# Local and global attention with a gated layer behind it: who normalises the probabilities of batches 2 to 7

## The chip, the cores and the metric

The kernel runs on one core of one Trainium2 chip. The core has five engines with a queue each, which work through their instructions in order: TensorE (PE, its weight loads PEld), VectorE (DVE), ScalarE (ACT), GpSimd (POOL) and SyncE (SP), which here issues every DMA. What counts is the time of one execution in microseconds on the device; lower is better.

## The reference

Per batch and head (8 x 8, head size 64), 512 local queries attend to 32 global keys and to the local keys within 32 positions; 32 global queries attend to all 544 keys. The softmax has an epsilon of 1e-9 in its denominator. The rows of all heads are put side by side (512 numbers for each of 4352 tokens) and go through a layer of width 2048:

```
def _moe_ref(x, w_in, w_out):
    h = x @ w_in
    g = h * np.cos(h)
    return g @ w_out
```

Inputs and result are fp32.

## The kernel before

**Two planes.** TensorE is fed with 16-bit floats. Every fp32 operand is scaled and split in two of them, a high plane (the rounded value) and a low plane (the remainder), and a product is three matmuls: high by high, high by low, low by high.

**The matrix layer** runs over 17 chunks of 256 tokens (`c`; two per batch, and a last one for the global queries of all batches), each in 8 slots (`j`), 136 slots in all. In a slot, 24 matmuls make `ph` (L877, 128 x 512 in PSUM, three buffers); ACT and DVE reduce the angle (`u`, L899 and L900); ACT takes the sine (`w`, L421), POOL squares it in place (L912), DVE makes `gf` from it and `ph` (L914), ACT casts its high plane `gh` (L918), POOL subtracts for the low plane `gl` (L919). Three slots later twelve matmuls (L933 to L935; L935 is the one that reads `gl`) add the result into two tiles `po`, one for each 128 tokens. At the end of a chunk ACT copies out the first `po` (L943) and DVE the second (L941), and SP writes them. A `ph` tile needs the buffer that the `gf` three slots earlier has read.

**The attention** of later batches runs in the same stretch, in pairs of heads: four pairs per batch, one in every four slots, so that the normalising of pairs 0 and 2 falls to slot 0 of a chunk and that of pairs 1 and 3 to slot 4. For a pair SP loads q and k (`qkr`, one buffer, L432), DVE takes their maximum (L472), TensorE spreads it (L454), ACT and DVE make the planes (`qa` L511, `kl` L512), SP copies halves of them (L521 to L526). The scores of four tiles of 128 queries come by TensorE (L579, L580); DVE scales them, adds the mask and takes the minimum (L596, two heads separately); ACT takes exponentials in place in `t` and sums them into `sm` (L421). Then `sc_d` normalises the four tiles and writes their planes into four fixed buffers `planes`, SP transposes these (`pt`, L688), and TensorE multiplies with the planes of v (L721; `vh` L569, `vl` L570, `vr` loaded at L439, its maximum at L540). Every second pair also has the global queries' scores (`gt`, `planes_g` L799, `ptg` L803). The result becomes `xh` (L745) and `xl` (L746), input of the matrix layer one batch later.

`sc_d` has several ways to normalise, chosen by a number: batch 0 by a list per tile, batch 1 by `PL1` (3), later batches by `PL` (1).

**Order.** The program writes the steps in an order by slot and phase; the tool that builds the kernel then reorders the instructions of each engine's queue by a timeline of its own. So a changed instruction can move others.

Of the kernel before, what the change touches and what calls it, by code (L numbers as in the profile page):

```python
# [45 lines left out]
SB = 2.0**14  # L46
T0 = 3
QB = 0
PL = 1
MF = 1  # L50
TS = 1
CH = ''
# [81 lines left out]
def body(tc, qk, v, wi, wo, mask, out):  # L134
# [5 lines left out]
    with ExitStack() as ctx:  # L140
# [504 lines left out]
        def sc_d(b, p, i):  # L645
# [3 lines left out]
            w = WIN[i][1]  # L649
            pl = PLS[i] if b == 0 else (PL0, PL1, PL)[min(b, 2)]  # L650
            if b < 2 and DEFN[b]:
# [504 lines left out]
```

## Time and profile before

| | |
|---|---|
| median of 3 runs | 1051.38 us (1048.57 to 1051.77) |
| the profiled execution | 1045.26 us, its span 1043.5 us |
| PE busy | 879.3 us (84%) |
| DVE busy | 729.4 us (70%) |
| ACT busy | 707.9 us (68%) |
| POOL busy | 463.1 us (44%) |
| granted TensorE clock, mean | 0.941 |

The profile is of one execution. A group's row reads: line, engine, operation, output <- inputs, output shape <- input shape, count, then total busy time and mean ns of one, then the idle time before such instructions and what ended it. A row of the timeline starts with its start and its length in us; the idle time before it and its releaser stand in brackets. Batches 0 and 1 of the attention, the loads and the splitting of the weights fill the first 250 us or so; from there to 884 us batches 2 to 7 run beside chunks 1 to 12, and the rest is matrix layer alone.

### The profile page before, as it was taken

The numbers are of one execution on the slowest core, as the hardware profiler recorded it, in microseconds if no ns is written. First come the engines' busy times: TensorE is split into PE (matmuls) and PEld (weight loads), VectorE is DVE, ScalarE is ACT, GpSimd is POOL, SyncE is SP. The second block draws the span as 40 slices with busy tenths as digits, with TensorE's granted clock in tenths as the row PEclk, the third lists the DMA queues.
The fourth block names the chain that finished last, engine by engine and source line by source line (L and its number), as shares of the span: only waits on it lengthen the run. The fifth ranks groups of instructions, "written<-read, shape, count | busy, mean of one in ns | idle before, by whom it ended". The sixth has DMA issues, their size and how long they took to land.

```text
span 1043.5 us, 20761 instructions
## 1 busy us (share of the span) xinstructions
PE 879.3 (84%) x7819; PEld 600.3 (58%) x7819; DVE 729.4 (70%) x1797; ACT 707.9 (68%) x1458; POOL 463.1 (44%) x396
## 2 busy tenths in 40 slices
PE   2133558677999999999899998999889999999996
PEld 1112435455566666666666666666667676666663
DVE  5997598999577777786777777877777766433231
ACT  6676478887378776877677667876777777434342
POOL 4885285957334342434233333333334333444442
PEclk9955679887999999999999999999999999999998
DMA  9869622796464546354553545455555442200000
GB/s 368 213 202 218 179 99 89 157 178 127 115 131 89 130 83 162 86 122 90 155 106 94 116 123 108 111 107 145 106 105 102 110 85 63 46 21 21 1 21 21
DMA packets 181565, 120.18 MB, mean 115 GB/s; under 512 B 159832, under 2 KB 159832, under 8 KB 179416
## 3 DMA queue, kind: packets, MB, share of 16 engines
q1 hardware_dynamic: 181464, 118.85, 47.6%
q8 instruction: 61, 1.00, 0.4%
q14 instruction: 40, 0.33, 0.1%
HBM read 51.81 MB, written 8.91 MB: 58 GB/s over the span
## 4 chain that ended last, share of the span: by engine, by line
DVE 36%; PE 29%; DMA 14%; ACT 11%; issue 6%; POOL 2%; SPq 1%; ACTq 0%; DVEq 0%; POOLq 0%
PE ph L877 12%; DMA qkr<-qk 6%; DVE t L596 5%; DVE planes L676 5%; PE po L933 5%; PE po L935 5%; PE po L934 5%; DVE u L900 4%; DMA vr<-v 3%; DVE gf L914 3%; ACT L421 3%; DVE kl L512 2%; DVE qm L472 2%; PE acc L721 2%; DVE vl L570 2%
## 5 line engine op out<-in xcount | busy, mean ns | idle before, releaser
L877 PE MATMUL ph<-xh,wi_h 128*128 128x256 f16 x1024 | 281.8, 276 | 31.1 <-DVE gf L914 31.1
L877 PE MATMUL ph<-xl,wi_h 128*128 128x256 f16 x1024 | 282.3, 276 | 0.0
L877 PE MATMUL ph<-xh,wi_l 128*128 128x256 f16 x1024 | 282.2, 276 | 0.0
L919 POOL TENSOR_TENSOR gl<-gf,gh 128x512 f16<-128x512 f32 x136 | 165.1, 1218 | 234.0 <-ACT gh L918 233.6
L912 POOL TENSOR_TENSOR w<-w 128x512 f32<-128x512 f32 x136 | 145.6, 1075 | 266.5 <-ACT w L421 254.5
L877 PEld LDWEIGHTS <-wi_h 128*128 128x128 f16 x2176 | 211.6, 99 | 68.1 <-DVE gf L914 18.4
L933 PE MATMUL po<-wo_h,gh 128*128 128x512 f16 x544 | 206.9, 384 | 21.3 <-DVE o L941 17.7
L934 PE MATMUL po<-wo_l,gh 128*128 128x512 f16 x544 | 207.2, 381 | 0.6 <-POOL wo_l L268 0.6
L935 PE MATMUL po<-wo_h,gl 128*128 128x512 f16 x544 | 206.9, 381 | 0.0
L421 ACT ACTIVATE w<-u,ca 128x512 f32<-128x512 f32 x136 | 97.0, 721 | 112.6 <-DVE u L900 112.2
L900 DVE SCALAR_TENSOR_TENSOR u<-u,cm,ph 128x512 f32<-128x512 f32 x136 | 100.0, 742 | 97.1 <-ACT u L899 97.0
L421 ACT ACTIVATE t<-t,mn 128x192 f32<-128x192 f32 (+1 forms) x256 | 117.1, 458 | 59.3 <-DVE mn L596 58.8
L918 ACT CAST gh<-gf 128x512 f16<-128x512 f32 x136 | 83.1, 611 | 78.0 <-DVE gf L914 70.6
L914 DVE SCALAR_TENSOR_TENSOR gf<-w,ph 128x512 f32<-128x512 f32 x136 | 92.5, 681 | 55.2 <-POOL w L912 55.0
L877 PEld LDWEIGHTS <-wi_l 128*128 128x128 f16 x1088 | 107.6, 99 | 15.7 <-issue 2.0
L596 DVE CUSTOM_DVE_ANT_0 t<-ps,msk,al 128x192 f32<-128x192 f32 (+1 forms) x256 | 99.5, 426 | 10.4 <-PE ps L580 10.3
L899 ACT ACTIVATE u<-ph,cm 128x512 f32<-128x512 f32 x136 | 92.1, 677 | 16.5 <-PE ph L877 16.5
L934 PEld LDWEIGHTS <-gh 128*128 128x128 f16 x544 | 53.4, 98 | 69.6 <-issue 21.2
L676 DVE SCALAR_TENSOR_TENSOR planes<-t,sm,planes 128x192 f16<-128x192 f32 (+1 forms) x192 | 83.9, 489 | 10.7 <-ACT planes L673 10.7
L935 PEld LDWEIGHTS <-gl 128*128 128x128 f16 x544 | 53.4, 98 | 64.3 <-issue 1.7
L933 PEld LDWEIGHTS <-gh 128*128 128x128 f16 x544 | 53.2, 98 | 54.0 <-issue 5.3
L421 ACT ACT_TABLE_LOAD x57 | 73.1, 1283 | 1.0
(183 smaller groups left out, 1428.4 us busy)
## 6 DMA issues: line engine op xcount, KB each, us to landing
qkr<-qk SPq DMA_DIRECT2D x29, 608.0 KB, 4.6
vr<-v SPq DMA_DIRECT2D x8, 1280.0 KB, 7.8
kh<-qa SPq DMA_DIRECT2D x62, 152.0 KB, 2.6
out<-o SPq DMA_DIRECT2D x34, 256.0 KB, 2.6
qa<-kl SPq DMA_DIRECT2D x31, 152.0 KB, 3.7
kl<-kl SPq DMA_DIRECT2D x31, 152.0 KB, 4.7
wo_h<-wi SPq DMA_DIRECT2D x4, 1024.0 KB, 7.9
raw_wi<-wi SPq DMA_DIRECT2D x4, 1024.0 KB, 10.7
```

Of the source, the lines that this page charges most:

```text
L421: ins = nc.scalar.activation(*a, **k).ins
L596: nc.vector.tensor_tensor_reduce(t[:, h], pt[:, h], msk[:, MOFF[i] : MOFF[i] + w], al, 3.0e38, ALU.add, ALU.min, mn[:, h : h + 1],)
L676: nc.vector.scalar_tensor_tensor(lo, t[:, h], r, hi, op0=ALU.mult, op1=ALU.subtract)
L877: nc.tensor.matmul(ph[:, a], w[:, kc, f], x[:, kc, q], start=first and ip == 0, stop=last and ip == 2, skip_group_check=True,)
L899: nc.scalar.activation(u, ph, AF.Identity, bias=m)
L900: nc.vector.scalar_tensor_tensor(u, u, m, ph, op0=ALU.subtract, op1=ALU.subtract)
L912: nc.gpsimd.tensor_tensor(w, w, w, op=ALU.mult)
L914: nc.vector.scalar_tensor_tensor(gf, w, 0.5, st.pop(("ph", c, j)).rearrange("p a b -> p (a b)"), op0=ALU.subtract, op1=ALU.mult,)
L919: nc.gpsimd.tensor_tensor(gl, gf, gh, op=ALU.subtract)
L933: nc.tensor.matmul(po[k], gh[:, q], wo_h[:, f], start=(f == 0), stop=False)
L934: nc.tensor.matmul(po[k], gh[:, q], wo_l[:, f], start=False, stop=False)
L935: nc.tensor.matmul(po[k], gl[:, q], wo_h[:, f], start=False, stop=(f == NJ - 1))
```

## The change

One number: batches 2 to 7 take way 3 of `sc_d`, as batch 1 does, instead of way 1.

```diff
-PL = 1
+PL = 3
```

What `sc_d` does for a tile of `w` = 192 or 224 keys and two heads, cut to the two ways (`rr` holds the reciprocals of the sums):

```
649  w = WIN[i][1]
...
653  if pl in (0, 3, 4, 5):
654      if pl == 3:
655          r = rr[:, 2 * i : 2 * i + 2]
656          rb = bass.AP(tensor=r.tensor, offset=r.offset, ap=[r.ap[0], (1, 2), (0, w)])
657          nc.gpsimd.tensor_tensor(t, t, rb, op=ALU.mult)
...
665      (nc.scalar.copy if pl != 5 or HIE[i] else nc.vector.tensor_copy)(hi, t)
666      nc.gpsimd.tensor_tensor(lo, t, hi, op=ALU.subtract)
667  else:
668      for h in range(2):
...
673          nc.scalar.activation(hi, t[:, h], AF.Identity, scale=r)
...
676          nc.vector.scalar_tensor_tensor(lo, t[:, h], r, hi, op0=ALU.mult, op1=ALU.subtract)
```

Way 1 was, for each head, one ACT operation (L673: times the reciprocal, high plane) and one DVE operation (L676: times the reciprocal, less the high plane). Way 3 is, for both heads at once, a POOL multiplication in place (L657), an ACT cast (L665) and a POOL subtraction (L666). Over 6 batches, 4 pairs and 4 tiles that is 192 operations less on DVE, 96 less on ACT (192 gone, 96 new) and 192 more on POOL. Nothing else in the program text differs; the queues' orders do, from slot 16 on.

The first place is slot 3 and 4 of a chunk (here chunk 8; pair 1 of batch 5 is normalised, and `t_1_0` to `t_1_2` are its tiles). POOL before:

```order
L912 TENSOR_TENSOR w_3_7817<-w_3_7817 128x512
L799 TENSOR_TENSOR planes_g<-gt_0_7550,planes_g 128x544
L919 TENSOR_TENSOR gl_3_7915<-gf_3_7917,gh_3_7914 128x512
L912 TENSOR_TENSOR w_4_7947<-w_4_7947 128x512
L912 TENSOR_TENSOR w_5_8028<-w_5_8028 128x512
```

POOL now, where the numbers behind the names are others for the same tiles:

```order
L657 TENSOR_TENSOR t_1_0_7498<-t_1_0_7498,sm_1_7849 128x384
L657 TENSOR_TENSOR t_1_1_7585<-t_1_1_7585,sm_1_7849 128x448
...
L912 TENSOR_TENSOR w_3_7765<-w_3_7765 128x512
L799 TENSOR_TENSOR planes_g<-gt_0_7502,planes_g 128x544
L666 TENSOR_TENSOR planes_76<-t_1_0_7498,planes_76 128x2x192
...
L666 TENSOR_TENSOR planes_82<-t_1_2_7722,planes_82 128x2x192
L912 TENSOR_TENSOR w_4_7895<-w_4_7895 128x512
L919 TENSOR_TENSOR gl_3_7863<-gf_3_7865,gh_3_7862 128x512
L912 TENSOR_TENSOR w_5_7972<-w_5_7972 128x512
```

The four multiplications stand before w_3, the four subtractions before w_4, and gl_3 behind w_4. (Beside the even pairs, at slot 0, the multiplications stand behind w_7. For pair 0 then come gl_7, the four subtractions, w_0, w_1 and gl_0; for pair 2 w_0, a subtraction, gl_7, three subtractions, gl_0, w_1.) DVE at the same place, before:

```order
L512 SCALAR_TENSOR_TENSOR kl_3_8053<-qkr_3_7779,qs_3_7893,qa_3_8052 128x1216
L914 SCALAR_TENSOR_TENSOR gf_3_7917<-w_3_7817,ph_3_7791 128x512
L676 SCALAR_TENSOR_TENSOR planes_76<-t_1_0_7546,sm_1_7901,planes_76 128x192 x2
...
L900 SCALAR_TENSOR_TENSOR u_4_7946<-u_4_7946,cm_7476,ph_4_7921 128x512
L900 SCALAR_TENSOR_TENSOR u_5_8027<-u_5_8027,cm_7476,ph_5_8002 128x512
...
L914 SCALAR_TENSOR_TENSOR gf_4_7998<-w_4_7947,ph_4_7921 128x512
L914 SCALAR_TENSOR_TENSOR gf_5_8061<-w_5_8028,ph_5_8002 128x512
L900 SCALAR_TENSOR_TENSOR u_6_8090<-u_6_8090,cm_7476,ph_6_8065 128x512
L472 TENSOR_REDUCE qm_0_8225<-qkr_0_8125 128x1
```

DVE now:

```order
L512 SCALAR_TENSOR_TENSOR kl_3_7997<-qkr_3_7727,qs_3_7841,qa_3_7996 128x1216
L900 SCALAR_TENSOR_TENSOR u_4_7894<-u_4_7894,cm_7428,ph_4_7869 128x512
L596 ISA t_2_0_7915,mn_2_0_7916<-ps_2_0_7910,msk,al_2_7415 128x192
...
L914 SCALAR_TENSOR_TENSOR gf_3_7865<-w_3_7765,ph_3_7739 128x512
L472 TENSOR_REDUCE qm_0_8169<-qkr_0_8069 128x1
L900 SCALAR_TENSOR_TENSOR u_5_7971<-u_5_7971,cm_7428,ph_5_7946 128x512
L448 TENSOR_SCALAR d_qk_0_8171<-ident,qm_0_8169 128x128
...
L914 SCALAR_TENSOR_TENSOR gf_4_7942<-w_4_7895,ph_4_7869 128x512
L900 SCALAR_TENSOR_TENSOR u_6_8034<-u_6_8034,cm_7428,ph_6_8009 128x512
```

L676 is gone; u_4 and the next pair's score reductions (L596) stand before gf_3, and L472, the maximum over the next q and k, stands before u_5 and gf_4. On SP the load behind L472 moved as well: it stood behind the transposes of the pair's planes and stands now before them, right behind the copies `kh`.

The second place is TensorE around the product of tile 3. Before, its twelve matmuls stood together ahead of `ph_7`. Now:

```order
L933 MATMUL po_1_7769<-wo_h,gh_3_7862 128x512
...
L934 MATMUL po_1_7769<-wo_l,gh_3_7862 128x512
...
L579 MATMUL ps_2_2_8052<-kh_2_7594,qa_2_7590 128x224
...
L721 MATMUL acc_1_8122<-pt_1_8057,vh_1_7403 64x128
...
L877 MATMUL ph_7_8079<-xh_6288,wi_h 128x256
...
L877 MATMUL ph_7_8079<-xl_6289,wi_h 128x256
...
L935 MATMUL po_0_7768<-wo_h,gl_3_7863 128x512
```

Four of the twelve come first; then four score matmuls, eleven of the attention's product (`acc_1`, which stood behind the product of tile 4), and two of `ph_7`; the remaining eight, four of which read gl_3, come behind those.

The third place is DVE before the chunk boundary in the chunk of pair 2 (here chunk 9). Before:

```order
L914 SCALAR_TENSOR_TENSOR gf_1_8494<-w_1_8389,ph_1_8363 128x512
...
L512 SCALAR_TENSOR_TENSOR kl_0_8424<-qkr_0_8125,qs_0_8235,qa_0_8423 128x1216
...
L570 SCALAR_TENSOR_TENSOR vl_2_9443<-vr_8176,vs_8350,vh_2_9442 128x640
L900 SCALAR_TENSOR_TENSOR u_2_8523<-u_2_8523,cm_7476,ph_2_8498 128x512
L472 TENSOR_REDUCE qm_1_8662<-qkr_1_8560 128x1
L941 TENSOR_SCALAR o_1_8541<-po_1_7821,co_7477 128x512
```

Now:

```order
L512 SCALAR_TENSOR_TENSOR kl_0_8364<-qkr_0_8069,qs_0_8179,qa_0_8363 128x1216
...
L570 SCALAR_TENSOR_TENSOR vl_2_9375<-vr_8120,vs_8290,vh_2_9374 128x640
L914 SCALAR_TENSOR_TENSOR gf_1_8434<-w_1_8329,ph_1_8303 128x512
L900 SCALAR_TENSOR_TENSOR u_2_8463<-u_2_8463,cm_7428,ph_2_8438 128x512
L941 TENSOR_SCALAR o_1_8481<-po_1_7769,co_7429 128x512
...
L472 TENSOR_REDUCE qm_1_8602<-qkr_1_8500 128x1
```

gf_1 moved behind the last L570, and L941 ahead of L472. In the chunk of pair 0, L472 still stands ahead of L941, and gf_0 moved ahead of L512.

## The prediction

> **What bounds the kernel now.** I read the view by windows first. Batches 2 to 7 of the attention, where the change lies, run beside the matrix chunks between 250 and 884 us; behind that stand chunks 13 to 16 alone. The row gives the stretch, the busy time (and count) of PE, its weight loads, DVE, ACT and POOL, then the granted clock and the DMA share.
>
> ```profile
> 250.00:884.00 634.00, 602.07 (x5600) 413.59 (x5600) 465.70 (x1221) 465.49 (x995) 232.00 (x205) 0.99 0.50 111
> ```
>
> TensorE is busy 602.07 of 634 us at full clock. So 31.9 us is all that any relief of DVE and ACT can win here, and POOL is the idlest engine (37%). Next I read the waits between 260 and 900 us (line waited for, total us, times, longest), because they say where those 31.9 us lie.
>
> ```profile
> PE po L933 <- DVE o L941: 17.7, 11, 2.7
> PE ph L877 <- DVE gf L914: 10.6, 8, 1.5
> DVE qm L472 <- DMA qkr<-qk: 43.1, 20, 3.4
> ```
>
> Two places hold 28.3 us of it. The first is the chunk boundary: the second half of a new chunk's `po` needs the old one copied out by DVE (L941), and DVE stands in front of it at the maximum over the next q and k (L472), which waits for their load. The second is the pair of `ph` tiles 6 and 7 of some chunks: they need the `ph` buffers of tiles 3 and 4, which are free once DVE has made gf_3 and gf_4 (L914). The timeline of one even chunk (8) shows the second:
>
> ```profile
> 624.62 2.33 DVE L512 SCALAR_TENSOR_TENSOR kl<-qkr,qs,qa 128x1216 f16<-128x1216 f32 x1 [1.68 <-ACT qa L511]
> 626.88 0.67 DVE L914 SCALAR_TENSOR_TENSOR gf<-w,ph 128x512 f32<-128x512 f32 x1
> 627.60 0.27 PE L877 MATMUL ph<-xh,wi_h 128*128 128x256 f16 x1 [1.53 <-DVE gf L914]
> 634.59 0.28 PE L877 MATMUL ph<-xh,wi_h 128*128 128x256 f16 x1 [1.23 <-DVE gf L914]
> 633.84 0.69 DVE L914 SCALAR_TENSOR_TENSOR gf<-w,ph 128x512 f32<-128x512 f32 x1 [0.56 <-POOL w L912]
> 634.79 0.57 SPq L432 DMA_DIRECT2D qkr<-qk  x1
> ```
>
> Every `ph` tile 6 and 7 is that close. In chunks 4, 6, 8 and 10 TensorE waits there; in the other eight (chunk 9 below) it has about 2.2 us in hand for gf_3 (678.86 to 681.10) and 0.85 for gf_4 (685.85 to 686.70):
>
> ```profile
> 678.19 0.67 DVE L914 SCALAR_TENSOR_TENSOR gf<-w,ph 128x512 f32<-128x512 f32 x1
> 681.10 0.27 PE L877 MATMUL ph<-xh,wi_h 128*128 128x256 f16 x1
> 685.16 0.69 DVE L914 SCALAR_TENSOR_TENSOR gf<-w,ph 128x512 f32<-128x512 f32 x1 [0.57 <-POOL w L912]
> 686.70 0.27 PE L877 MATMUL ph<-xh,wi_h 128*128 128x256 f16 x1
> ```
>
> **Prices.** Batch 1 already runs the new form, so its operations stand in the trace (groups of 160 to 260 us for POOL, of the whole run for ACT and DVE):
>
> ```profile
> L657 POOL TENSOR_TENSOR t<-t,sm 128x448 f32<-128x448 f32 x8 | 7.9, 1003 | 0.0
> L657 POOL TENSOR_TENSOR t<-t,sm 128x384 f32<-128x384 f32 x8 | 7.3, 918 | 2.7 <-DVE sm L643 2.7
> L666 POOL TENSOR_TENSOR planes<-t,planes 128x384 f16<-128x384 f32 x8 | 10.4, 1294 | 1.0 <-ACT planes L665 1.0
> L666 POOL TENSOR_TENSOR planes<-t,planes 128x448 f16<-128x448 f32 x8 | 9.6, 1208 | 0.0
> L665 ACT CAST planes<-t 128x448 f16<-128x448 f32 x16 | 8.7, 558 | 0.0
> L673 ACT ACTIVATE planes<-t,sm 128x224 f16<-128x224 f32 x96 | 38.0, 466 | 0.0
> L676 DVE SCALAR_TENSOR_TENSOR planes<-t,sm,planes 128x192 f16<-128x192 f32 (+1 forms) x192 | 83.9, 489 | 10.7 <-ACT planes L673 10.7
> L919 POOL TENSOR_TENSOR gl<-gf,gh 128x512 f16<-128x512 f32 x136 | 165.1, 1218 | 234.0 <-ACT gh L918 233.6
> ```
>
> For each of 24 pairs (four tiles), DVE loses eight operations of 0.489, 3.9 us (83.9 in all by the row, where they overlap a little), and ACT exchanges two activations of 0.466 for one cast of 0.558, four times. POOL gains four multiplications (2 x 0.918 + 2 x 1.003 = 3.84 us) and four subtractions (2 x 1.294 + 2 x 1.208 = 5.00 us), 212 us in all, so it goes from 232 to some 444 of 634 us (70%). No engine's total passes TensorE's. What counts is where the blocks of 3.84 and 5.00 us stand in POOL's queue, since w (L912) feeds gf and gl (L919) feeds the second product; and what the changed orders do. The orders are those shown under the change.
>
> **Odd pairs (1 and 3), beside gf_3 and gf_4.** The reciprocal of the sums is ready at 621.45 and POOL is idle then:
>
> ```profile
> 621.25 0.20 DVE L643 RECIPROCAL sm<-sm 128x8 f32<-128x8 f32 x1
> 623.46 1.04 POOL L912 TENSOR_TENSOR w<-w 128x512 f32<-128x512 f32 x1 [8.54 <-ACT w L421]
> qkr<-qk SPq DMA_DIRECT2D x29, 608.0 KB, 4.6
> 664.74 0.38 PE L934 MATMUL po<-wo_l,gh 128*128 128x512 f16 x1
> 664.96 0.38 PE L935 MATMUL po<-wo_h,gl 128*128 128x512 f16 x1
> 346.83 1.29 PE acc L721 x36
> ```
>
> Multiplications to 625.3, w_3 to 626.3 (now 624.5), planes_g to 627.5, subtractions to 632.5, w_4 to 633.6, gl_3 to 634.8. On DVE L512 ends at 626.9 as now, but the new order puts u_4 (0.7, of L941's kind and size) and two score reductions (0.7 together, of half that size each) ahead of gf_3: it ends at 628.9, not 627.5, and the wait at 627.60 grows from 1.53 to 2.9 us. Behind gf_3 now stands L472, which used to come after gf_4 and gf_5. SP issues its load right after L512 (627.0) instead of 634.79, and it lands 4.6 later, 631.6; L472 runs to 633.0, u_5 to 633.7, the two d (0.2 each) and two reductions to 634.8 (w_4 is there by then), gf_4 to 635.5 instead of 634.5. TensorE begins `ph` tile 7 at 635.5, 0.9 later than 634.59. Its own order changes too: two of that tile's matmuls stand before eight of the twelve matmuls of the product of tile 3, so these 8 x 0.22 = 1.7 us (the step from L934 to L935 above) come after the wait instead of before it, and only four scores and eleven of the 36 matmuls of the attention's product fill their place: 11/36 of 1.29 is 0.4, and I give the scores as much, 0.9 with the two. Cost: 0.9 + 1.7 - 0.9 = **1.7 us in each of 4 chunks, +6.8**. In the other eight the same delays (gf_4 to 686.6, inside TensorE's former start) leave the displaced product alone: 1.7 - 0.9 = **0.8 each, +6.4**. From nothing, if the load lands sooner than the median, to 2.5 each.
>
> The gap of 2.9 us has a second price. After the 2.50 us gap below, the granted clock was 0.50 (second row). The longest gap of the stretch, the third row, is the only other one that long, and the clock's mean of 0.99 over the whole stretch leaves room for few more.
>
> ```profile
> 558.57 0.38 PE L933 MATMUL po<-wo_h,gh 128*128 128x512 f16 x1 [2.50 <-DVE o L941]
> 559.00:561.00 2.00, 2.00 (x9) 0.58 (x9) 1.05 (x4) 1.87 (x6) 0.22 (x1) 0.50 0.57 176
> 773.01 0.38 PE L933 MATMUL po<-wo_h,gh 128*128 128x512 f16 x1 [2.68 <-DVE o L941]
> ```
>
> Half clock lasts at least the 2 us of that row, which loses 1.0 of work; a mean of 0.99 (0.985 to 0.995) over 634 us is 3.2 to 9.5 us of full clock lost, 1.6 to 4.8 for each of two. I take 1.7 for one, near the end that a row shows, and two of the four gaps of 2.9: **+3.4** (none to four at 1.7: 0 to 6.8). The Trainium skill, "TensorE: Matmul & The Clock Gate", Part 1, puts the drop after an idle window of about 3.4 us that runs freely; by it alone a gap of 2.9 would cost nothing and the sum would be 3.4 lower. The trace's 2.50 us gap speaks against that reading.
>
> **Even pairs, before the chunk boundary.** Pair 2 first, at the boundary of chunk 9:
>
> ```profile
> 648.14 1.04 POOL L912 TENSOR_TENSOR w<-w 128x512 f32<-128x512 f32 x1 [3.60 <-PE gps L762]
> 659.11 1.51 DVE L512 SCALAR_TENSOR_TENSOR kl<-qkr,qs,qa 128x1216 f16<-128x1216 f32 x1
> 664.76 1.42 DVE L472 TENSOR_REDUCE qm<-qkr 128x1 f32<-128x1216 f32 x1 [0.98 <-DMA qkr<-qk]
> 666.10 0.74 DVE L941 TENSOR_SCALAR o<-po,co 128x512 f32<-128x512 f32 x1
> 666.89 0.38 PE L933 MATMUL po<-wo_h,gh 128*128 128x512 f16 x1 [1.56 <-DVE o L941]
> ```
>
> L941 now stands ahead of L472, so it no longer waits for a load. But gf_1 has moved behind L570, and POOL reaches w_1 only after its blocks: w_7 to 649.2, multiplications to 653.0, w_0, one subtraction, gl_7, three subtractions to 660.2, gl_0, w_1 to 662.5. Then gf_1, u_2 and L941 end at 664.5, 2.3 earlier than now. ACT's copy of the first half stands behind gh_1 and ends at 664.5 too, where TensorE wanted it at 663.9 (five steps of 0.22 before its L935 at 664.96). So a wait of 0.6 to 0.8 stays. Five of the eleven waits that sum to 17.7 are such, among them the two long ones quoted above; by the same timeline they come to 10.1. 5 x 0.8 stay: **-6.1** (none to all of it), and the half clock behind two of them goes: **-3.4**.
>
> At the boundaries after pair 0 L472 stays ahead, and the new order puts gf_0, and with it w_0, before L512, while POOL runs gl_7 and all four subtractions before w_0. On the timeline above that is, from the end of w_7 at 649.2: 3.84 + 1.2 + 3.8 (subtractions undisturbed, 0.95 each) to 5.0, + 1.04 for w_0 and 0.7 for gf_0, so 659.8 to 661.0; today L512 starts at 659.1, and the load and L941 hang on it. So 0.7 to 1.9 later; multiplications undisturbed would take some of it back, and I take 0.7 at **5 boundaries, +3.5** (0 to 9).
>
> What else is late (gf_0 to gf_2, gl_7, gl_0, the planes' transposes, each by 2 to 6 us) is used a slot or more later, behind at least the 24 matmuls of a `ph` tile and twelve of a product; without that cover each would cost what it is late. At the start of batch 2 TensorE has the first products to do; I take 0, within 2 either way.
>
> **Sum:** 6.8 + 6.4 + 3.4 - 6.1 - 3.4 + 3.5 = 10.6, **+11 us**. The profiled execution took 1045.26 us, its span is 1043.5; it lies 6.1 below the median of the runs, 1051.38. The same +11 on the median gives **1062 us**.
>
> **Rivals.** *Faster.* L941 is freed at both kinds of boundary, since DVE has 3.9 us less work per pair, and the earlier load removes its wait beside the odd pairs: 17.7 us of waits and 3.4 of half clock go, the odd pairs cost 6: -15, 1036 us. For it: 43.1 us of L472's waits, and that the load leaves SP 7.8 us sooner. Against it: TensorE's new order itself places gl_3 behind other work, and L472 now stands before gf_4. Chance 0.22.
>
> *Nothing.* The same terms, the odd pairs costing half: 1048 to 1054.5. Chance 0.17.
>
> *Slower still, by contention of POOL with DVE.* The rows (min/median/max):
>
> ```profile
> L512 DVE SCALAR_TENSOR_TENSOR kl<-qkr,qs,qa x28: 1468/1874/2462, 138.1 to 834.2; 128x1216 f16<-128x1216 f32 x28
> L570 DVE SCALAR_TENSOR_TENSOR vl<-vr,vs,vh x24: 871/1388/1670, 208.3 to 819.2; 128x640 f16<-128x640 f32 x24
> L472 DVE TENSOR_REDUCE qm<-qkr x24: 1402/1419/1422, 213.8 to 823.1; 128x1 f32<-128x1216 f32 x24
> ```
>
> With POOL at work on most of the even pairs' stretch, L512 and two L570 would stand near their longest: 0.99 + 2 x 0.8 = 2.6 us later L941 at 10 boundaries. It decides as soon as subtractions are still running when L512 starts; it takes back the 9.5 won and adds 5 to 10, about +25: 1076 us. Against it: the mean prices above hold part of it already. Chance 0.14. The Trainium skill, "GPSIMD Engine Reference", Key points, says that POOL shares its SBUF interfaces with VectorE and collides with instructions of two SBUF inputs. L512 and L570 have two and vary, L472 has one and is constant: the trace agrees.
>
> That the change does nothing is excluded: POOL has 192 instructions more in the order.
>
> **How the numbers follow.** The forecast itself (1054.5 to 1075) has 0.47. About 0.3% is what a measurement here can tell from no change (1048.2 to 1054.5). Faster 0.22, same 0.17, slower 0.47 + 0.14 = 0.61. The likeliest case's own range is 1053 to 1071 (no half clock and cheap odd pairs; four half clocks and w_0 at its latest). For eight in ten: 1044 to 1078, which leaves out most of the fast rival and the tail of contention.
>
> **What would show it.** Right: POOL 660 to 690 us busy; TensorE's waits for gf_3 and gf_4 in all twelve chunks, or for gl_3 right behind; waits for L941 shorter at the boundaries after pair 2, unchanged after pair 0; more half-clock stretches near `ph` tile 6. Wrong: PE busy over 610 us of the same work's stretch with no wait at gf_3, or L472 landing before gf_3 is done, or L941 waits gone everywhere; then the fast rival holds.

## The result and the profile after

The changed kernel takes 1057.68 us (median of 8 runs, 1054.15 to 1061.56); the kernel before takes 1048.63 us in as many runs beside it (1045.81 to 1051.77). The ratio is 1.0102, with a 95% interval of 1.0075 to 1.0128: slower by about 10.7 us (the two medians lie 9.1 apart). Forecast were +11 us. The sum came out, but by luck. The experiments below show that its main place, the order of the queues beside the odd pairs, is right; but a gain of some 15 us beside the odd pairs, which it left out, stood against the even pairs, which cost about 8 us where it had them win 6.

The profiled execution after is one of 1054.15 us with a span of 1052.4. The first 250 us are equal in both (slot 16 of the matrix layer, the first of chunk 2, starts at 250.6 us in either trace), and the end from chunk 14 on takes 143.7 us in both; the whole difference of 8.9 us arises between, in chunks 2 to 13. (Chunks are counted from 0; these are the ones beside which batches 2 to 7 run, not 1 to 12 as said above.) By the view by windows (stretch and length, then the busy time and count of PE, its weight loads, DVE, ACT, POOL, then granted clock, DMA share and GB/s), for the stretch that answers to 250 to 884 us, and for one piece out of it:

```profile
250.00:893.00 643.00, 608.49 (x5606) 415.41 (x5606) 411.71 (x1036) 444.94 (x903) 425.58 (x394) 0.99 0.49 109
414.60:417.90 3.30, 3.30 (x17) 2.31 (x16) 1.05 (x1) 0.69 (x2) 3.30 (x5) 0.50 0.82 169
```

DVE went from 466 to 412 us and ACT from 465 to 445, POOL from 232 to 426 (660 us in the whole span; the prediction said 660 to 690). Neither relief shows in the time. The half clock has moved: the pieces of 3.41 us behind the boundaries at 558.57 and 773.01 are gone, and there is one beside the odd pair in each of the chunks 4, 6, 8 and 10 (the first is shown). TensorE's waits of the changed kernel between 260 and 910 us:

```profile
PE ph L877 <- DVE gf L914: 10.9, 9, 2.1
PE acc L721 <- DMA pt<-planes: 9.7, 8, 3.0
PE po L933 <- DVE o L941: 6.6, 5, 1.6
PE pm_qk L454 <- DVE d_qk L448: 5.5, 5, 1.7
```

The first row has hardly moved (10.6 before). The wait for L941 fell from 17.7 to 6.6 us, and two rows are new: the attention's product waits for the transposed planes (no row before), and TensorE stands at L454, the spread of the maximum over q and k (0.2 before). Together TensorE's waits between 256 and 905 us grew by 2.4 us and the time lost at half clock by 3.4, so these rows explain about 6 of the 8.9 us. The groups of the changed kernel in the same stretch (POOL's new work, then what POOL and DVE do beside it):

```profile
L666 POOL TENSOR_TENSOR planes<-t,planes 128x384 f16<-128x384 f32 x46 | 48.2, 1049 | 0.0
L657 POOL TENSOR_TENSOR t<-t,sm 128x448 f32<-128x448 f32 x47 | 48.1, 1043 | 0.0
L666 POOL TENSOR_TENSOR planes<-t,planes 128x448 f16<-128x448 f32 x46 | 46.8, 1036 | 0.0
L657 POOL TENSOR_TENSOR t<-t,sm 128x384 f32<-128x384 f32 x46 | 38.0, 827 | 38.2 <-DVE al L491 33.4 <-DVE sm L643 4.8
L912 POOL TENSOR_TENSOR w<-w 128x512 f32<-128x512 f32 x91 | 110.5, 1217 | 55.3 <-ACT w L421 54.9
L512 DVE SCALAR_TENSOR_TENSOR kl<-qkr,qs,qa 128x1216 f16<-128x1216 f32 x22 | 39.4, 1791 | 11.5 <-ACT qa L511 11.5
L570 DVE SCALAR_TENSOR_TENSOR vl<-vr,vs,vh 128x640 f16<-128x640 f32 x21 | 28.6, 1381 | 0.4 <-ACT vh L569 0.4
```

The four rows of POOL sum to 181 us (the prediction had 212 from batch 1's rows). In the same view of the kernel before L512 has a mean of 1965 ns and L570 one of 1212, so one is shorter, the other longer, and the two together take what they took (68 us). POOL is slowed: L912 takes 1.22 us where it took 1.06 (1058 ns).

How the new waits arise shows the timeline of chunk 8 (pair 1 of batch 5; start, length):

```profile
624.52 3.79 POOL L657 TENSOR_TENSOR t<-t,sm 128x384 f32<-128x384 f32 x4 [4.87 <-DVE al L491]
628.27 2.22 POOL L912 TENSOR_TENSOR w<-w 128x512 f32<-128x512 f32 x1
631.62 3.77 POOL L666 TENSOR_TENSOR planes<-t,planes 128x384 f16<-128x384 f32 x4
635.35 1.04 POOL L912 TENSOR_TENSOR w<-w 128x512 f32<-128x512 f32 x1
633.87 1.42 DVE L472 TENSOR_REDUCE qm<-qkr 128x1 f32<-128x1216 f32 x1 [2.34 <-DMA qkr<-qk]
635.20 0.73 DVE L900 SCALAR_TENSOR_TENSOR u<-u,cm,ph 128x512 f32<-128x512 f32 x1
638.25 0.68 DVE L914 SCALAR_TENSOR_TENSOR gf<-w,ph 128x512 f32<-128x512 f32 x1
631.69 2.35 SPq L803 DMA_TRANSPOSE ptg<-planes_g  x1
634.14 5.55 SPq L688 DMA_TRANSPOSE pt<-planes  x4
638.60 0.30 PE L721 MATMUL acc<-pt,vh 128*64 128x128 f16 x4 [3.00 <-DMA pt<-planes]
```

POOL begins the four subtractions at 631.62 and ends them at 635.35. SP issues the four transposes one after the other from 634.14 to 639.7; the first, whose plane was ready by 632.6, stood for 1.5 us behind the transpose of `planes_g` (L803). TensorE, which under the new order meets the first eleven matmuls of the attention's product right behind the first four of the product of tile 3 and four score matmuls, stands there for 3.00 us. On DVE, L472 waits 2.34 us for its load with u_5 and gf_4 behind it. POOL had w_4 ready at 636.39; gf_4 starts at 638.25, so here DVE's queue sets it, not POOL.

### The profile page after: what moved, and what is told of

The parts are those of the page before. It is cut to its first block, busy times and chain, and to the rows that moved or that the text cites. A ratio compares the mean times of both kernels' runs of the same rounds, so it can differ in the third digit from the quotient of the medians.

```text
span 1052.4 us, 20658 instructions
## 1 busy us (share of the span) xinstructions
PE 884.3 (84%) x7819; PEld 600.5 (57%) x7819; DVE 673.7 (64%) x1605; ACT 686.1 (65%) x1362; POOL 659.7 (63%) x588
## 4 chain that ended last, share of the span: by engine, by line
PE 37%; DVE 22%; POOL 13%; DMA 12%; issue 10%; ACT 4%; SPq 1%; POOLq 0%; DVEq 0%; ACTq 0%
PE ph L877 15%; PE po L935 6%; PE po L934 6%; PE po L933 6%; POOL planes L666 5%; DMA qkr<-qk 4%; DMA vr<-v 3%; POOL t L657 3%; DVE t L596 3%; POOL w L912 2%; POOL gl L919 2%; DMA pt<-planes 2%; DVE kl L512 2%; PE acc L721 2%; DVE u L900 1%
## 5 line engine op out<-in xcount | busy, mean ns | idle before, releaser
L919 POOL TENSOR_TENSOR gl<-gf,gh 128x512 f16<-128x512 f32 x136 | 169.4, 1250 | 165.6 <-ACT gh L918 165.4
L912 POOL TENSOR_TENSOR w<-w 128x512 f32<-128x512 f32 x136 | 160.4, 1182 | 108.0 <-ACT w L421 107.5
L933 PE MATMUL po<-wo_h,gh 128*128 128x512 f16 x544 | 206.2, 383 | 11.2 <-DVE o L941 6.6
L657 POOL TENSOR_TENSOR t<-t,sm 128x384 f32<-128x384 f32 (+1 forms) x120 | 110.9, 954 | 52.3 <-DVE al L491 33.4
L666 POOL TENSOR_TENSOR planes<-t,planes 128x448 f16<-128x448 f32 (+1 forms) x128 | 135.5, 1087 | 1.6 <-ACT planes L665 1.6
L596 DVE CUSTOM_DVE_ANT_0 t<-ps,msk,al 128x192 f32<-128x192 f32 (+1 forms) x256 | 99.6, 426 | 10.4 <-PE ps L580 10.1
L933 PEld LDWEIGHTS <-gh 128*128 128x128 f16 x544 | 53.3, 98 | 53.6 <-issue 5.9
```

Source lines behind the costliest of these rows:

```text
L596: nc.vector.tensor_tensor_reduce(t[:, h], pt[:, h], msk[:, MOFF[i] : MOFF[i] + w], al, 3.0e38, ALU.add, ALU.min, mn[:, h : h + 1],)
L657: nc.gpsimd.tensor_tensor(t, t, rb, op=ALU.mult)
L666: nc.gpsimd.tensor_tensor(lo, t, hi, op=ALU.subtract)
L912: nc.gpsimd.tensor_tensor(w, w, w, op=ALU.mult)
L919: nc.gpsimd.tensor_tensor(gl, gf, gh, op=ALU.subtract)
L933: nc.tensor.matmul(po[k], gh[:, q], wo_h[:, f], start=(f == 0), stop=False)
```

## The experiments

Each number below is the median of the kernel's runs and the ratio to the kernel before on the same chip, with its 95% interval.

**The pairs apart.** Two kernels have the new form for the even pairs or for the odd ones; around the others DVE's queue stands as before.

```diff
-            pl = PLS[i] if b == 0 else (PL0, PL1, PL)[min(b, 2)]
+            pl = PLS[i] if b == 0 else (PL0, PL1, PL if p % 2 == 0 else 1)[min(b, 2)]
```

(The second has `p % 2 == 1`.)

> The new form for pairs 0 and 2 alone; pairs 1 and 3 keep the old form, and the queues around them keep the order of before. Theory (odd pairs cost, even pairs gain): the waits at the boundaries after pair 2 fall from 10.1 to about 5 us, the two stretches at half clock behind them go (3.4), nothing else moves: about 8 us faster than before, 1040 us. Rival (each pair costs the same, by POOL colliding with the other engines): half of the whole change's 9 us, so about 4.5 slower than before, 1053 us.

> The new form for pairs 1 and 3 alone. Theory: all that the change costs lies here: 4.7 more of waits for gf in chunks 4, 6, 8 and 10, 5 of new waits for the transposed planes in the other chunks, four stretches at half clock (6.8), so about 16 us slower than before, 1065 us, while the waits for L941 at the boundaries stay near 17.7. Rival (the same cost per pair): 1053 us.

Even pairs alone: 1049.22 us, 1.0028 (1.0002 to 1.0054). Odd pairs alone: 1050.51 us, 1.0029 (1.0012 to 1.0046). The theory of a gain at the even pairs and a loss of 16 us at the odd ones falls; by the medians the rival, the same small loss on each side, is nearer, and the two sum to 0.57%, each a quarter per cent uncertain or less, against 1.02% for the whole change. The prediction's own terms sum to +16.6 us beside the odd pairs and -6.0 beside the even ones; measured are +3.0 for the odd pairs alone, and +7.7 for the even ones on top of them. The waits of TensorE between 256 and 905 us, even pairs alone:

```profile
PE po L933 <- DVE o L941: 12.5, 5, 3.1
PE po L933 <- ACT o L943: 10.5, 8, 1.9
PE pm_qk L454 <- DVE d_qk L448: 6.4, 8, 2.4
```

Odd pairs alone:

```profile
PE ph L877 <- DVE gf L914: 15.8, 10, 2.5
PE acc L721 <- DMA pt<-planes: 8.9, 10, 1.8
PE po L933 <- DVE o L941: 6.0, 8, 1.1
```

With the even pairs alone the wait at the boundary is not won but grows (17.7 to 23.0 us together): after pair 2 it is now ACT's copy (L943, behind gh_1) that is late, as the prediction said of that copy, but by 1.6 to 1.9 us rather than 0.8, and after pair 0 L941, which waits for w_0, gf_0 and L512, by 2.0 to 3.1 us. In the whole change this wait is 6.6 us; that TensorE comes to the boundary later, because of the odd pairs, and finds most of it over, is my reading and not shown by a run. With the odd pairs alone the wait at the boundary falls to 6.0 us though L472 stands ahead of L941 as before: the relief of DVE, TensorE's delay or both are enough for that. The waits at gf_3 in chunks 4, 6, 8 and 10 are 2.3 to 2.5 us there, near the 2.9 of the prediction.

**The swap alone.** The kernel before, with one order fixed on DVE:

```diff
+                if p % 2 and b * 4 + p > 10:
+                    tc.add_manual_dep(q.ins, st["oc"].name, order, reason="program_order")
```

The other engines' queues stay as they are, but for two neighbours on ACT that change places in each chunk (gh_2 and u_3).

> The kernel before, with the old form everywhere; only DVE's order at the chunk boundaries is changed: L941 ahead of L472 (as the change has it after pair 2, here after pair 0 too). Theory (the gain of the even pairs is this swap and not the work taken from DVE): the 17.7 us of waits for L941 go, a wait of about 1 us for the spread maximum (L454) takes their place at each of 11 boundaries, and the two stretches at half clock go: 6 + 3.4, about 9 us faster, 1039 us. Rival (L472's lateness sets the next pair as much as L941 sets the product): within 2 us of before, 1047 to 1051.

1040.98 us, 0.9944 (0.9907 to 0.9981): faster, by 6 to 7 us where 9 were expected.

```profile
PE ph L877 <- DVE gf L914: 10.0, 9, 1.5
PE pm_qk L454 <- DVE d_qk L448: 7.3, 11, 1.6
PE ps L579 <- DVE mn L596: 7.0, 4, 2.4
PE po L933 <- DVE o L941: 0.7, 1, 0.7
```

The 17.7 us at L941 are gone but for 0.7. In their place TensorE waits 7.3 us at L454, as expected, and 7.0 us at the scores (L579) in chunks 4, 6, 8 and 10, which was not: there DVE stands at L540 for the load of v, with u_3 and the score reductions behind it. So L941's place is worth something by itself, and most of the wait comes back at the next things behind it.

**TensorE's order.** The changed kernel with two orders fixed: `ph` tile 7 behind all of the product of tile 3, and the attention's product of an odd pair behind the product of tile 4. No other queue changes by a row.

```diff
+                    if 2 <= c < 14 and j == 7 and first and ip == 0:
+                        tc.add_manual_dep(mm.ins, st["m2", c, 3].name, order, reason="program_order")
...
+                        if b >= 2 and p % 2 and k + ip + h == 0:
+                            tc.add_manual_dep(mm.ins, st["m2", 2 * b - 2 + p // 2, 4].name, order, reason="program_order")
```

> The changed kernel with TensorE's order of before beside the odd pairs: ph tile 7 behind the whole product of tile 3, the attention's product behind that of tile 4; the other queues are as in the changed kernel. Theory (the order is a cause of its own): the 10 us of waits for the transposed planes go; what comes in their place is a wait of 1 to 2 us for gl_3 in four to twelve chunks, short enough to keep full clock in part; 4 to 12 us faster than the changed kernel, 1046 to 1053 us. Rival (POOL is late, whatever TensorE does first): the wait only changes its name, 1056 to 1060 us.

1056.43 us, 1.0076 (1.0044 to 1.0107): 0.26% less than the changed kernel, inside the uncertainty of either. The wait changed its name, as the rival said:

```profile
PE po L935 <- POOL gl L919: 11.7, 10, 2.0
PE po L933 <- DVE o L941: 7.2, 5, 1.9
PE pm_qk L454 <- DVE d_qk L448: 7.0, 5, 2.0
PE ph L877 <- DVE gf L914: 4.7, 3, 2.5
```

The planes have left the list, and gl_3, behind w_4 and the subtractions on POOL, has taken their place.

**TensorE's and DVE's order.** As the last, and on DVE beside the odd pairs u_4 behind gf_3 and L472 behind u_6:

```diff
+                if p % 2 == 0 and b * 4 + p > 9:
+                    tc.add_manual_dep(q.ins, st["uj", 6].name, order, reason="program_order")
...
+            st["uj", j] = nc.vector.scalar_tensor_tensor(u, u, m, ph, op0=ALU.subtract, op1=ALU.subtract).ins; (c > 1 and j == 4) and tc.add_manual_dep(st["uj", 4], st["gf3"].name, order, reason="program_order")
```

With it the builder itself puts gl_3 ahead of w_4 on POOL and gh_3 ahead of w_4 on ACT, as before. I call this the order of before beside the odd pairs, though two things in it stay as in the changed kernel: two score reductions (L596) stand ahead of gf_3, and SP issues the load for L472 right behind L512.

> The changed kernel with the order of before beside the odd pairs on both TensorE (as in the run before this) and DVE (u_4 behind gf_3, L472 behind u_6); POOL, SP and the even pairs stay as changed. Theory (POOL's blocks are late, whoever waits for them): still 5 to 10 us slower than before, 1053 to 1058 us, the waits at gf and gl_3 beside the odd pairs together within 4 us of those of the changed kernel at gf and pt. Rival (DVE's new order, with L472 and its load ahead of gf_4, is what costs): 1046 to 1050 us.

1039.36 us, 0.9928 (0.9903 to 0.9954). The theory that POOL's blocks are late whoever waits for them falls; the rival holds, and by more than it said: with the order of before beside the odd pairs the same operations are 7.5 us *faster* than the kernel before, 18 us faster than the changed one. SP's early load may have a part in it, which no run takes out: beside the odd pairs it is issued 0.03 to 0.5 us after L512's end (7.0 to 8.0 in the kernel before), and L472, which stands late again, no longer waits for it (2.4 to 3.4 us each before).

```profile
PE pm_qk L454 <- DVE d_qk L448: 7.5, 5, 2.4
PE po L933 <- DVE o L941: 6.8, 5, 1.9
PE po L935 <- POOL gl L919: 5.1, 4, 1.3
PE ph L877 <- DVE gf L914: 3.8, 4, 1.8
```

**POOL's time and DVE's relief.** In the first of two kernels POOL's two operations work on an eighth of the columns for batches 2 to 7; the rest stays unnormalised and its low plane is what was there. In the second, the kernel before, L676 is left out for these batches, so the probabilities have no fresh low plane. In both the builder also shifts rows, on DVE too.

```diff
-                    r = rr[:, 2 * i : 2 * i + 2]
+                    r, z = rr[:, 2 * i : 2 * i + 2], w // 8 if b > 1 else w
...
-                    nc.gpsimd.tensor_tensor(t, t, rb, op=ALU.mult)
+                    nc.gpsimd.tensor_tensor(t[:, :, :z], t[:, :, :z], rb, op=ALU.mult)
...
-                nc.gpsimd.tensor_tensor(lo, t, hi, op=ALU.subtract)
+                nc.gpsimd.tensor_tensor(*(x if pl != 3 else x[:, :, :z] for x in (lo, t, hi)), op=ALU.subtract)
```

```diff
-                    nc.vector.scalar_tensor_tensor(lo, t[:, h], r, hi, op0=ALU.mult, op1=ALU.subtract)
+                    b > 1 or nc.vector.scalar_tensor_tensor(lo, t[:, h], r, hi, op0=ALU.mult, op1=ALU.subtract)
```

> The changed kernel with POOL's multiplications and subtractions of batches 2 to 7 on an eighth of the columns (the other columns stay unnormalised and their low plane old); the same number of instructions, ACT and DVE as changed; beside the odd pairs the queues fall back to the order of before. Theory (the time that POOL's blocks take is the cost): all of the loss goes and some of DVE's relief is seen, 1038 to 1048 us. Rival (the new form costs by its steps and order, not by POOL's time): 1053 us or more.

> The kernel before without L676 for batches 2 to 7 (the low plane of the probabilities is left out): DVE has 84 us less and nothing is put in its place; TensorE's order is unchanged. Theory (what TensorE waits for at DVE is a load and a place in the queue, not DVE's amount of work): the waits at L941 shrink by less than half, 1043 to 1048 us. Rival (DVE's work is what is late): the 28 us of waits go by two thirds, 1030 us.

The first took 1031.63 us, 0.9857 (0.9813 to 0.9901). That is all of the loss and more, as the theory has it, but it is not POOL's time alone: TensorE's, L472's and u_4's places beside the odd pairs are again those of before, and so is DVE's order at the boundary after pair 2. Against the kernel of the last run, which has TensorE's, L472's and u_4's places too, it is 0.7% faster, half a per cent uncertain; how much of that is POOL's time isn't shown. The second took 1022.86 us, 0.9768 (0.9724 to 0.9812): 24 us faster. My theory is wrong there. Taking 84 us from DVE removes two thirds of what TensorE waits for, at places where the releaser's name was a load or L941's place in the queue:

```profile
PE po L933 <- DVE o L941: 5.4, 4, 1.6
PE pm_qk L454 <- DVE d_qk L448: 2.3, 3, 1.1
PE ph L877 <- DVE gf L914: 2.1, 2, 1.1
```

Of the 31 us in the kernel before, 10 remain. At the boundary the cause can be read from the traces. L472 stands ahead of L941 in both kernels, and in both SP issues the load that L472 waits for 0.03 us after L512's end, and L472 starts 3.6 to 5.1 us after that end. So the load was late because DVE was. The wait at L941 fell from 17.7 to 5.4 us with L472 still ahead of it. Beside the odd pairs it is less clean: there the builder also put gf_4 ahead of two score reductions.

**The swap on the changed kernel.** L941 ahead of L472 after pair 0 too; DVE's order alone, but for the same two neighbours on ACT.

> The changed kernel with L941 ahead of L472 after pair 0 as well (DVE's order alone; after pair 2 it stands so already). Theory (the boundary after pair 0 waits for w_0, gf_0 and L512, which POOL's block delays, as much as for L472): the 6.6 us of waits for L941 fall to about 2 and a wait at L454 of about 1 us takes their place, 1 to 3 us faster than the changed kernel, 1055 us. Rival (the swap is worth here what it was worth in the kernel before, 7 us over 11 boundaries): about 3 us more of gain, 1051 us.

1056.77 us, 1.0084 (1.0062 to 1.0105): within 0.2% of the changed kernel, near the theory's 1055. The wait for L941 is gone, and the waits at gf and at the planes (10.9 and 10.0 us between 256 and 905 us in the changed kernel) have grown:

```profile
PE ph L877 <- DVE gf L914: 15.3, 11, 2.5
PE acc L721 <- DMA pt<-planes: 12.0, 9, 1.9
```

What TensorE does not wait for at the boundary it waits for at the odd pair behind it. So the boundary does not set the pace there.

**L472 alone, and with TensorE's order.** Two kernels take the orders apart. The first moves only L472 and the two small instructions behind it on DVE (every other queue is that of the changed kernel, row by row); the second adds TensorE's order of before.

> The changed kernel; on DVE alone, beside the odd pairs, L472 (the maximum over the next q and k) and the two small instructions that need it stand behind u_6 again, as before; TensorE, POOL, SP and ACT are in the order of the changed kernel to the last instruction. Theory (L472 stands waiting for its load ahead of u_5, gf_4 and all that follows them, and this is what the change costs): the waits at gf fall by half or more and the wait for the transposed planes shrinks too, 10 us or more faster than the changed kernel, 1042 to 1047 us. Rival (the place of L472 counts only together with TensorE's order, since the product that waits for the planes stands in front): 1051 to 1057 us.

> The changed kernel with TensorE's order of before and L472's place of before beside the odd pairs; u_4 stays ahead of gf_3, and the other queues are in the order of the changed kernel to the last instruction. Theory (with L472 out of the way the product that waits for the planes is the next thing in front of ph tile 7, so TensorE's order is worth more here than the 3 us that it was worth alone): as fast as with u_4 moved back too, 1038 to 1042 us. Rival (the two places only add up, 9 and 3 us, and the rest was u_4 and the score reductions ahead of gf_3): 1045 to 1048 us.

L472 alone: 1050.67 us, 1.0016 (0.9989 to 1.0042), 0.86% or 9 us less than the changed kernel; its runs lie further apart than any other kernel's, 1042.99 to 1055.71. The median lies between what the theory and the rival said. In its profiled execution, which is the fastest one, the waits at gf are 5.7 us (10.9 in the changed kernel) and those at the planes 11.6 (10.0), so the first half of the theory holds and the second does not. Both: 1046.03 us, 0.9990 (0.9968 to 1.0013). So 0.86% for L472's place and 0.26% for TensorE's order add up (1.0102 - 0.0086 - 0.0026 = 0.9990, closer than the uncertainty of each lets one expect), as the rival had it. The step from there to 0.9928 is u_4 ahead of gf_3 on DVE, with gh_3 behind w_4 on ACT and gl_3 behind w_4 on POOL, which moved along. The score reductions stand ahead of gf_3 in both kernels and are no part of it.

**Which pairs the new form suits.** Both have TensorE's and DVE's order of before beside the odd pairs, as above; the first has the new form for pairs 1 and 3, the second for 1, 2 and 3.

```diff
+            pl = PLS[i] if b == 0 else (PL0, PL1, PL if p % 2 else 1)[min(b, 2)]
```

```diff
+            pl = PLS[i] if b == 0 else (PL0, PL1, PL if p else 1)[min(b, 2)]
```

> The new form for pairs 1 and 3 alone, with the order of before on TensorE and DVE beside them. Theory (the even pairs cost some 5 us wherever the odd ones stand, as their own run showed): 5 us less than the kernel with both and these orders, 1034 us. Rival (with the odd pairs in order, DVE's relief at the even pairs is a gain): 1042 us or more.

> The new form for pairs 1, 2 and 3, the old one for pair 0 alone, with the order of before on TensorE and DVE beside the odd pairs. Theory (the prediction's: at the boundary after pair 2 the new form gains, since L941 gets ahead of L472; only pair 0 costs): faster than the odd pairs alone, 1028 to 1032 us. Rival (both even pairs cost, pair 2 by the wait at L454 and by w_1 and gf_1 standing behind POOL's block, about half of the 6 us each): 1035 to 1038 us.

Odd pairs: 1033.73 us, 0.9851 (0.9822 to 0.9880), the fastest kernel here that computes all that the one before does, 1.5% faster than it. Pairs 1, 2 and 3: 1038.17 us, 0.9919 (0.9883 to 0.9954). The theory holds for the first and the rival for the second. Pair 2 in the new form costs 0.7%, half a per cent uncertain, so the prediction's gain at that place has the wrong sign; pair 0 on top (0.9928) costs nothing that can be measured. The waits of the odd pairs alone, with the orders, and SP's load for L472 at the boundary of chunk 9:

```profile
PE po L933 <- DVE o L941: 8.0, 10, 1.7
PE ph L877 <- DVE gf L914: 7.3, 4, 2.2
PE pm_qk L454 <- DVE d_qk L448: 0.6, 1, 0.6
652.45 0.34 SPq L432 DMA_DIRECT2D qkr<-qk  x1
```

and of pairs 1, 2 and 3:

```profile
PE ph L877 <- DVE gf L914: 8.6, 4, 2.2
PE pm_qk L454 <- DVE d_qk L448: 6.5, 6, 2.3
PE po L933 <- DVE o L941: 4.0, 6, 1.1
662.04 0.59 SPq L432 DMA_DIRECT2D qkr<-qk  x1
```

Pair 2's new form brings L941 ahead of L472, wins 4.0 us at L933 and loses 5.9 at L454, where TensorE waits for what comes of L472. L472 is late not by its place alone: without the new form SP issues its load 0.03 us after L512's end (652.42 in chunk 9), with it only 4.5 to 5.7 us after (656.86 in chunk 9), behind the last transpose of the planes that POOL now makes. And two more stretches at half clock (three, where the other has one) cost 1.7 us each.

## Why the prediction was right, and where it was not

From the kernel before to the changed one the runs give this ladder (each step is uncertain by 0.35 to 0.45%, 4 to 5 us, so those of pair 0 and of TensorE's order could be nothing):

| kernel | ratio | step, of 1048 us |
|---|---|---|
| before | 1 | |
| odd pairs new, order of before on TensorE and DVE | 0.9851 | -15.6 |
| and pair 2 | 0.9919 | +7.1 |
| and pair 0 | 0.9928 | +0.9 |
| and u_4 ahead of gf_3, gh_3 and gl_3 behind w_4 | 0.9990 | +6.5 |
| and TensorE's new order | 1.0016 | +2.7 |
| and L472 with its load ahead of u_5 and gf_4: the change | 1.0102 | +9.0 |

- **"What counts is where the blocks stand in POOL's queue, and what the changed orders do."** Right: the three new orders beside the odd pairs cost 18 us, while everything else in the change wins 7.5. With the odd pairs alone the same orders cost as much (1.0029 against 0.9851, 18.7 us). The step names the rows that the runs then moved: u_4 ahead of gf_3, L472 ahead of gf_4, TensorE's displaced product. Its price for them, 16.6 us with the half clock, is near the 18. Of the three only L472's place is shown to cost something by a run that moves it alone; TensorE's order by itself could be nothing, and u_4 never moved alone.
- **The odd pairs, +6.8 and +6.4.** The place was right; in the trace the four chunks 4, 6, 8 and 10 lose 4.7 us more to waits and the others 5.3. But the form of the loss was another. The waits at gf_3 did not grow from 1.53 to 2.9: by TensorE's rows those of the four chunks are 1.98, 0.73, 0.92 and 2.05, in sum what they were (with the odd pairs alone they did grow, to 2.3 to 2.5). The wait is at the transposed planes, 9.7 us. The step that failed is that eleven matmuls of the attention's product would fill the place of the displaced ones: they need planes that POOL makes late and SP transposes one after the other. The same holds of "what else is late ... the planes' transposes ... is used a slot or more later": that was read from the old order and is not so in the new.
- **Half clock, +3.4.** In the profiled execution four stretches instead of two of four, so 6.8, mis-sized by half; that the two behind the boundaries go (-3.4) was right. What decides is told below; it isn't the single gap of 2.5.
- **Even pairs, pair 2: -6.1.** In the trace of the change L941's wait after pair 2 falls from 10.1 us to nothing, more than said, and 5.5 come at L454 instead. The prediction took L472 out of L941's way and did not ask who waits for L472, nor when SP would now issue its load. By the runs the whole step costs 7.1 instead of winning 6.1 and the half clock.
- **Even pairs, pair 0: +3.5.** In the kernel with the even pairs alone TensorE waits there as worked out, and for longer (14.1 us over five boundaries by its rows, 12.5 of it at L941; 6.9 before). In the whole change the wait is 6.6 and nothing is lost: it may be that TensorE's delay at the odd pairs covers it. A delay at one place can be cover at the next; a sum of places counts both.
- **DVE's relief.** The step that failed most: the reading that 28.3 us lie at two places with their own releasers, so that 84 us less on DVE are worth only what those places give. Leaving L676 out wins 24 us, with the rows that the builder moved along. A wait that is put down to a load or to a place in the queue can still end with DVE's amount of work, since the load starts when L512 has freed its buffer. In the sum this missing gain (15.6 us beside the odd pairs, by the ladder) and pair 2 (+7.1 where -9.5 was forecast with the half clock, 16.6 off) cancelled: that +11 came out is luck, though the price of the orders came near.
- **The rivals.** "Faster" (-15) describes the odd pairs in the new form with DVE's and TensorE's order held; that its number is the one measured then is chance, since it was meant for the boundaries. SP's earlier load, which it named, may be part of that gain; no run takes it out. "Slower still, by contention": DVE's L512 and L570 together are not slower, so it fell. L570 alone is 0.17 us longer, and on POOL L912 is 0.16 us longer.

What stays open: between 0.9990 and 0.9928 several places changed together (u_4 on DVE, gh_3 on ACT, gl_3 on POOL, and L472 by two score reductions), and no run takes them apart; how the 7.5 us divide between DVE's relief and SP's earlier load; and pair 2's 7 us are shown, while waits and half clock account for about 5 of them in the traces.

## What to carry to other kernels

Where a tool orders the queues, a change of one operation is two changes, and the second can be larger: here -7.5 us with three orders held and +18 for those orders. Compare the queues before timing, and fix the order of what stands ahead of the critical instruction, a maximum that waits for a load above all; then judge the operations. When an instruction is moved out of another's way, price who waits for the one that now comes later. And when a wait ends with a load, look at what let the load start.

## What the runs showed of the hardware

The half clock keeps to a grid. In each trace all stretches at half clock start and end on multiples of 3.413 us from one another (the last is cut by the trace's end), and what decides is TensorE's idle time within one such window, not the length of a gap. Windows and the next ones, before:

```profile
500.93:504.34 3.41, 1.53 (x12) 0.62 (x12) 3.41 (x9) 3.09 (x13) 0.00 (x0) 1.00 1.01 279
504.34:507.75 3.41, 3.41 (x59) 3.13 (x56) 1.01 (x2) 1.85 (x3) 1.16 (x1) 1.00 0.72 266
555.54:558.95 3.41, 0.91 (x5) 0.32 (x4) 2.51 (x5) 2.98 (x10) 0.84 (x1) 1.00 0.47 131
558.95:562.36 3.41, 3.41 (x31) 1.84 (x31) 1.84 (x5) 2.21 (x6) 1.16 (x1) 0.50 0.34 105
```

and after, where the gaps in the first window are 1.50 us and part of one of 1.46:

```profile
527.21:530.62 3.41, 1.19 (x16) 0.81 (x16) 2.59 (x7) 1.29 (x3) 2.25 (x4) 1.00 1.01 192
530.62:534.03 3.41, 3.41 (x13) 1.51 (x10) 2.33 (x7) 2.50 (x4) 2.10 (x2) 0.50 0.46 91
```

A gap of 2.21 us at 500.6 lies partly in the window ahead and does nothing; a gap of 1.50 and 0.72 of another in one window halve the clock of the next. Over the fourteen traces of this case, between 256 and 900 us, 27 stretches begin from full clock; TensorE was idle for 1.91 to 3.06 us of the window ahead of each, and no window with less than 1.9 us idle is followed by one (from 1.90 to 2.00 both occur). So some 56% of a window is the point. The Trainium skill, "TensorE: Matmul & The Clock Gate", Part 1, has the free-running window of 3413 ns, which the traces show, and the drop after an idle window, which is more than the traces ask for: some 1.9 us of idleness in it are enough. That also answers the prediction's question between a rule of 3.4 us and the gap of 2.50: neither.

POOL is slowed beside DVE's L512: the squaring w_3, which is 1.04 us elsewhere, takes 2.22 us at 628.27 in the timeline above, while L512 runs from 627.61 to 629.59. So it is each time in that trace: in all eleven chunks in which L512 overlaps w_3 by 1.32 us, w_3 takes 2.22.
